# Attention and a feed-forward block on one core: the first two batches' q and k loaded in halves of 256 tokens, attention units of 192 tokens, the first chunk up-projected in column halves

## The chip, the cores and the metric

The kernel runs on one core of a Trainium2 chip. A core has a matrix engine (PE), a vector engine (DVE), a scalar engine (ACT), a general engine (POOL) and an engine that mostly issues loads and stores (SP). They run side by side, each through its own list of instructions in a fixed order, and wait for each other by semaphores. The metric is the device time of one execution in microseconds; less is better.

## The reference

Inputs are q, k and v (8 batches, 8 heads, 576 tokens, 64 per head, float32), w_in (512 x 2048) and w_out (2048 x 512).

```python
scores = scale * np.matmul(q, k.transpose(0, 1, 3, 2))
rel = pos[:, None] - pos[None, :]
mask_plain = (rel >= 0) & (rel < 32)
mask_dil = (rel >= 0) & (rel < 128) & (rel % 4 == 0)
# heads 0 to 3 take mask_plain, heads 4 to 7 mask_dil; softmax over the keys; times v
x = attn_out.transpose(0, 2, 1, 3).reshape(B * S, H * D)     # 4608 x 512
h = x @ w_in
out = np.maximum(0.01 * h, h) @ w_out                        # 4608 x 512, float32
```

Heads 0 to 3 ("plain", group 0) see the last 32 tokens, heads 4 to 7 ("dilated", group 1) every fourth of the last 128. Four tokens in a row are one step of the dilated heads, so all tokens of one residue modulo 4 attend among themselves.

## The kernel before

Everything is computed in float16 with float32 sums. The program is not written in the order in which it runs: every piece of work is handed to a small planner (`_Plan`, L62) as a task with an engine, an estimated duration, the tasks it depends on and a priority. `run` (L85) walks through time, gives each free engine the ready task of lowest priority number, and so fixes each engine's order; the instructions are then recorded in that order. Where the planner sees PE idle for over some 0.4 us in the head, matmuls on zeros are put in (L1595, after eight at the start, L1489): fillers, whose result nobody reads.

Attention is done batch by batch. Batches 0 and 1 (`EARLY`) take one path, the other six another one (`late_unit`, L945) which the change leaves as it is. On the early path `load_group` (L396) loads q and k of four heads, 512 tokens, with four tokens of one head (1 KB) as one piece and 128 partitions of four tokens; batch 0 in loads of two heads (256 KB), batch 1 in loads of four (512 KB). They land in float32 in the tiles `stg` and are cast into `nat` (L272). `turn` (L658) transposes them on PE (L692) into the bank `tp` or `fps`, and copies (L642, L644) bring them into `slots`: `qbd`, in which the two heads of a pair stand block-diagonally, and `kt`, the keys. The last 64 tokens of a batch follow by `load_rest` (L501), cast into `rest`.

A head pair of a batch is done in three units (`unit`, L807). Part 0 has the units 0 and 1, part 1 unit 2, with the last tokens. A plain unit covers 192 tokens in a row. A dilated unit 0 or 1 covers 96 steps of two residues, so that units 0 and 1 together need 384 tokens; unit 2 covers 48 steps of four residues. A unit's chain: a product on PE that adds the mask as a bias (L837, where `BY_PE` has the batch and part; elsewhere a mask is multiplied in afterwards on DVE or POOL, L874), the scores (L840 or L854), exp on ACT (L860), the product with the values and with ones (L886 to L918), the reciprocal as Ln and Exp on ACT (L930, L932) and the scaling into `xt` on DVE (L936). For batch 0's plain heads the values are loaded as they lie, cast into `pair` (the tile `pair1`), and brought into the windows that the units need by products with a spread identity (`permute`, L333).

`xt` holds x transposed, by chunks of 384 columns: for every two batches chunk 0 has the first 384 tokens of the even batch, chunk 1 those of the odd one, chunk 2 the last 192 of both. `up` (L1081) multiplies a chunk by w_in, 128 rows of the result at a time, four matmuls each (512 = 4 x 128), into one of two banks `hps`, and ACT writes it with the leaky ramp into `gt` (L1102). Chunk 0 is planned matmul by matmul (`BLOCKS`), so that it can begin before all of w_in is there. The rows 0 to 1023 of the result need the w_in blocks 0 to 3, the others the blocks 4 to 7. `down` (L1264, L1275) multiplies by w_out, and later `group` (L1315, L1364) does four tiles at once with seven products where eight would be plain.

Loads are issued by SP in the planner's order, which for the first two batches is given by the string `FIRST`: each sign is a group of loads (`b` q and k and `v` the values of a group of heads of batch 0, `c` and `y` of batch 1, `i` a block of w_in, `o` a block of w_out, 512 KB each, `0` and `1` the last tokens). Every load waits for the landing of the eighth load before it. `took` (L252) is the planner's estimate of a load's time, `LATE` what it adds to it for later loads, `AHEAD` how far it lets issues run ahead of the transfers, `RANKS` the priorities of the attention of the first two batches.

w_in and w_out arrive in float32 in tiles that are free early (`gt`, `wst`, `xt[1]`) and are cast in halves of 512 columns by `cast` (L265), on DVE or POOL; w_in's blocks 4 to 7 on POOL alone.

Of the kernel before, what the change touches and what calls it, by code (L numbers as in the profile page):

```python
# [9 lines left out]
FP16 = mybir.dt.float16  # L10
# [5 lines left out]
AHEAD, LATE = 5.0, 4.0  # L16
WHEN = (-5.0, 15.0, 46.0, 70.0, 100.0, 126.0, 160.0, 188.0)
CON = -1484.5
LOCK = 60.0
AFTER = -1495.0  # L20
FIRST = "bvbviiii0iiiicoocoyoooooy1"
RANKS = ((10.0, 6.0), (10.0, 0.5), (15.0, 2.0), (25.0, 2.0))


def _constants():
# [15 lines left out]
    d2 = (rel2 >= 0) & (rel2 < WIN)  # L41
    bias = np.where(np.concatenate([first, band, band, d0, d2], axis=1), 0.0, -60000.0)
    parts = [ident, bias, first, band, band, d0, d1, d1, d0, d2]
# [18 lines left out]
class _Plan:  # L62
# [22 lines left out]
    def run(self):  # L85
        free, waiting, lock = {}, {}, {}
        server = 0.0
# [12 lines left out]
        while len(order) < len(self.tasks):  # L100
            best = None
            for eng, cand in waiting.items():
# [3 lines left out]
                if eng == "SP":  # L106
                    here = max(here, server - AHEAD)
# [18 lines left out]
            if t.service:  # L126
                begin = max(at + t.dur + 0.9, server)
                server = begin + t.service
                t.done = server + 1.1 + t.late
            else:  # L130
                t.done = at + t.dur + t.lat
# [11 lines left out]
def kernel(  # L143
# [24 lines left out]
    TILED = ((0, 0), (0, 1), (1, 0))  # L168
    BY_PE = ((0, 0), (0, 1), (1, 0))
    POOL_MASK = (1,)  # L170
    BLOCKS = tuple(range(16))
    N_UPS = 8
# [20 lines left out]
    NBIAS, NMASK = 288 + 96 + 48, 288 + 288 + 48  # L193
# [3 lines left out]
    B_PL, B_D0, B_D2 = 128, 128 + 288, 128 + 288 + 96  # L197
# [47 lines left out]
    tpk = fps[1].bitcast(FP16)  # L245
# [6 lines left out]
    def took(n, size):  # L252
        for a, ta, b, tb in ((4, 9.0, 128, 15.0), (128, 15.0, 256, 19.0), (256, 19.0, 1024, 48.0),
                             (1024, 48.0, 2048, 85.0)):
            if size <= b:
                return n * (ta + (tb - ta) * (size - a) / (b - a)) / 16e3
        return n * size / 25.6 / 16e3

    def load(queue, dst, src, n, size, deps, prio, slow=1.0):
# [3 lines left out]
                        LATE if prio > -1500 + len(FIRST) else 0.8 if prio >= AFTER else 0.0)  # L263
# [35 lines left out]
    def clear_slots(slots, prio, deps):  # L299
        for i in slots:  # L300
            t_zero[i] = ([clear("DVE", qbd[i][64:128, 0:S], 0.34, 0.0, prio, deps),
                          clear("DVE", qbd[i][0:64, S:2 * S], 0.34, 0.0, prio, deps)],
                         [clear("DVE", kt[i][:, 0:PAD], 0.1, 0.0, prio, deps)])

    clear_slots(range(4), -2000, [])
    t_one = clear("POOL", ones, 0.1, 1.0, -1995)
    t_ones = {}
    TWO_ONES = float(np.ones(2, np.float16).view(np.float32)[0])

    def clear_ones(slots, deps, prio=-700):  # L310
        for i in slots:
            t_ones["d", i] = clear("POOL", at(vd[i].bitcast(FP32), 0, 128, D // 2, [64, 16], [1, D // 2]),
                                   0.48, TWO_ONES, prio,
                                   deps)
            t_ones["p", i] = clear("POOL", at(vp[i].bitcast(FP32), 0, 128, D // 2, [64, 12], [1, D // 2]),
                                   0.38, TWO_ONES, prio,
                                   deps)

    clear_ones(range(2), [], -1980)
    t_vr = [clear("POOL", vst[i][0:64, 1024:2048], 1.0, 0.0, -1970 + i) for i in range(2)]  # L320
    SPREAD, SHIFT = 36, 67

    def ident_at(tl, off, step, prio):
        t = clear("DVE", tl.bitcast(FP32), 0.3, 0.0, prio)
        return add("DVE", 0.2, 0.2, [t, t_id], lambda e: nc.vector.tensor_copy(
            out=at(tl, 0, 128, off, [step, 128]), in_=ident), prio)

    t_spread = ident_at(el[0], SPREAD, 4, -1985)
    t_shift = ident_at(el[1], SHIFT, 1, -1600)
    v_half = pair1  # L330
    permuted = []

    def permute(tiles, deps, prio, rest_from=None):  # L333

        if rest_from is None:
            n, b_users = tiles[0] // 2, []
            b_old = rings["TPK"][-1] if n else []
            bk = fps[n]
        else:
            n, b_old = ring("F", 2, b_users := [])  # L340
            bk = fps[n]

        def pe(e):
            for y, t in enumerate(tiles):
                for r in range(4):
                    s = 96 * t - 32 - r + SPREAD
                    nc.tensor.matmul(bk[:, 256 * y:256 * y + 256], el[0][:, s:s + 128],  # L347
                                     at(v_half, 0, 128, r * D, [256, 4], [1, D]),
                                     start=(y == 0 and r == 0), stop=(r == 3), skip_group_check=True)
                if t == 5:  # L350
                    for r in range(4):
                        for i in range(2):
                            nc.tensor.matmul(bk[:, 256 * y + 128 * i:256 * y + 128 * i + 128],
                                             el[1][0:64, 3 - r:131 - r],
                                             at(turned[i], 0, 64, r * D, [256, 2], [1, D]),
                                             start=False, stop=(r == 3), skip_group_check=True)
        t_p = add("PE", 0.11 * (4 * len(tiles) + 4 * (5 in tiles)), 0.25,
                  deps + b_old + [t_spread] + [t_shift] * (5 in tiles), pe, prio)
        permuted.append((t_p, b_users))
        res = []  # L360
        for j in range(2):
            vt = vp[j]

            def fn(e, j=j, vt=vt):
                o = at(vt, 0, 128, tiles[0] * 128, [768, 2], [128, 2], [1, D])
# [5 lines left out]
            t = add((("ACT", 0.3), ("DVE", 0.36)), None, 0.2, [t_p] + kept_old[j], fn, prio)  # L371
            b_users.append(t)
            res.append(t)
        if rest_from is None:
            rings["F"][n].extend(res)
# [4 lines left out]

    kept, v_late, seen_ones = {}, {}, {}
    kept_old = [[], []]

# [1269 lines left out]
```

## Time and profile before

| | |
|---|---|
| median of 3 runs | 306.08 us (305.56 to 306.25) |
| the profiled execution | 306.29 us, its span 304.50 us |
| PE busy | 294.4 us (97%), 2970 matmuls |
| DVE busy | 231.0 us (76%) |
| ACT busy | 188.7 us (62%) |
| POOL busy | 132.3 us (43%) |
| moved by DMA | 51.09 MB, 168 GB/s in the mean |

The span runs from the first to the last instruction; 1.79 us of the profiled execution lie around it. A busy PE is not always at useful work: the fillers count. The rows of a timeline have the start, the time from the first start to the last end of a run of like instructions, the engine, the line, the operation, what it writes and reads, and in brackets the idle time before it and what ended it. PE's matmuls overlap, so the pace of a run is read from the starts. SPq is SP issuing a load.

### The profile page before, as it was taken

The page shows a single profiled execution, that of the slowest core. Times are in us where ns is not written, and L with a number is a line of the kernel's source. Part 1 is how long each engine was busy: PE and PEld are TensorE (multiplying, and loading weights), DVE is VectorE, ACT ScalarE, POOL GpSimd, SP SyncE. Part 2 cuts the span into 40 slices and gives each one's busy share as a digit, 9 for nine tenths or more (in the row PEclk, how much of TensorE's full clock was granted, in tenths as well). Part 3 has the DMA queues.
Part 4 walks back from the last instruction along what each step waited for, and adds up shares of the span by engine and source line. Part 5 has one row for each costly group of instructions (what it writes and reads, how often), then busy time and mean ns, then how long its engine had stood idle before and what let it go on. Part 6 is the DMA issues. An engine that isn't in the chain of part 4 may idle for free.

```text
span 304.5 us, 7869 instructions
## 1 busy us (share of the span) xinstructions
PE 294.4 (97%) x2970; PEld 225.4 (74%) x2970; DVE 231.0 (76%) x478; ACT 188.7 (62%) x458; POOL 132.3 (43%) x179
## 2 busy tenths in 40 slices
PE   6889999999999999997999999999999999999994
PEld 3646655667777676786777777887788999999984
DVE  6875875689686869959888779879775899697552
ACT  3857854795556678464766567456565688767230
POOL 5469555393674949159094668665000000000000
PEclk9999999999999999999999999999999999999999
DMA  7999999999999899976999969793102110031124
GB/s 241 404 370 392 407 289 201 239 201 167 253 171 196 190 188 196 174 180 134 183 161 221 204 136 194 159 208 80 37 2 72 34 37 2 11 91 32 32 76 146
DMA packets 160390, 51.09 MB, mean 168 GB/s; under 512 B 137632, under 2 KB 157024, under 8 KB 160352
## 3 DMA queue, kind: packets, MB, share of 16 engines
q1 hardware_dynamic: 159520, 49.86, 68.3%
q10 hardware_dynamic: 832, 0.73, 0.8%
q8 instruction: 23, 0.38, 0.5%
q14 instruction: 15, 0.12, 0.1%
HBM read 41.13 MB, written 9.44 MB: 166 GB/s over the span
## 4 chain that ended last, share of the span: by engine, by line
PE 90%; DVE 5%; ACT 3%; DMA 1%; issue 1%; DVEq 0%
PE hps L1091 29%; PE fps L1364 26%; PE fps L1275 9%; PE ops L1015 3%; PE hps L1188 3%; PE ops L1188 3%; PE ops L1063 2%; PE sps L1188 2%; PE tp L1188 1%; PE tp L692 1%; PE ops L1364 1%; PE tp L982 1%; PE sps L982 1%; DVE ee L1008 1%; PE fps L347 1%; PE tp L975 1%
## 5 line engine op out<-in xcount | busy, mean ns | idle before, releaser
L1091 PE MATMUL hps<-xt,w_in 128*128 128x384 f16 (+1 forms) x640 | 111.7, 310 | 0.8 <-DVE w_in L272 0.6
L1102 ACT ACTIVATE gt<-hps 128x384 f16<-128x384 f32 (+1 forms) x160 | 72.8, 461 | 43.8 <-PE hps L1091 41.5
L1091 PEld LDWEIGHTS <-w_in 128*128 128x128 f16 x640 | 56.7, 98 | 26.3 <-DVE w_in L272 1.0
L1364 PEld LDWEIGHTS <-gt 128*128 128x128 f16 x672 | 64.4, 98 | 9.7
L679 POOL COPY slots<-turned 64x576 f16<-64x576 f16 x48 | 36.3, 757 | 47.4 <-DVE turned L674 45.5
L1364 PE MATMUL fps<-w_out,gt 128*128 128x256 f16 x416 | 53.6, 273 | 0.0
L272 POOL CAST nat<-stg 128x576 f16<-128x576 f32 (+1 forms) x53 | 43.0, 834 | 9.7 <-DMA stg<-in_q_dram 3.5
L1275 PE MATMUL fps<-w_out,gt 128*128 128x512 f16 x128 | 32.4, 379 | 0.0
L1037 DVE TENSOR_TENSOR rc<-ops,recs 96x384 f16<-96x384 f32 x48 | 25.7, 538 | 0.3
L1393 ACT COPY stg<-fps 128x512 f32<-128x512 f32 (+1 forms) x24 | 12.8, 532 | 14.4 <-PE fps L1364 14.4
L1008 DVE TENSOR_TENSOR ee<-ee,con 128x576 f16<-128x576 f16 x24 | 17.2, 722 | 3.5 <-ACT ee L994 3.5
L1033 DVE RECIPROCAL recs<-ops 96x6 f32<-96x6 f32 x48 | 8.7, 181 | 14.7 <-PE ops L1015 12.5
L1401 DVE TENSOR_TENSOR osb<-fps,stg 128x512 f32<-128x512 f32 x18 | 12.4, 687 | 9.7 <-PE fps L1364 5.6
L272 POOL CAST vd<-v_all 128x1024 f16<-128x1024 f32 (+2 forms) x20 | 18.0, 918 | 2.7 <-DMA v_all<-in_v_dram 2.7
L1211 ACT ACTIVATE gt<-stg 128x384 f16<-128x384 f32 x36 | 18.0, 524 | 1.1 <-DVE stg L1205 1.1
L1275 PEld LDWEIGHTS <-gt 128*128 128x128 f16 x128 | 11.6, 98 | 9.1
L644 DVE COPY slots<-tp 64x128 f16<-64x128 f16 (+7 forms) x42 | 13.4, 333 | 6.3 <-PE tp L692 5.6
L674 DVE STREAM_TRANSPOSE turned<-nat 128x576 f16<-128x576 f16 x24 | 17.7, 751 | 0.0
L685 DVE STREAM_TRANSPOSE slots<-nat 128x576 f16<-128x576 f16 x24 | 17.7, 745 | 0.0
L1008 DVE TENSOR_TENSOR el<-el,con 128x576 f16<-128x576 f16 x24 | 15.0, 630 | 2.7 <-ACT el L994 2.5
L1188 PEld LDWEIGHTS <-w_in 128*128 128x128 f16 x192 | 16.4, 98 | 0.5 <-DVE w_in L1119 0.3
L994 ACT ACTIVATE ee<-sps 128x288 f16<-128x288 f32 x24 | 9.8, 409 | 8.4 <-PE sps L982 5.8
(158 smaller groups left out, 529.3 us busy)
## 6 DMA issues: line engine op xcount, KB each, us to landing
stg<-in_q_dram SPq DMA_DIRECT2D x48, 144.0 KB, 3.2
stg<-in_k_dram SPq DMA_DIRECT2D x48, 144.0 KB, 2.9
v_all<-in_v_dram SPq DMA_DIRECT2D x24, 256.0 KB, 3.8
v_all<-in_v_dram SPq DMA_DIRECT2D x24, 192.0 KB, 3.2
gt<-in_moe_w_in_dram SPq DMA_DIRECT2D x5, 512.0 KB, 7.1
out_dram<-osb SPq DMA_DIRECT2D x22, 96.0 KB, 2.0
out_dram<-osb SPq DMA_DIRECT2D x40, 48.0 KB, 1.8
out_dram<-osb SPq DMA_DIRECT2D x25, 64.0 KB, 2.2
```

The costliest lines, as they stand in the source:

```text
L272: ENG[e].tensor_copy(out=dst, in_=src)
L674: lambda e: nc.vector.transpose(xb, na[:, 0:S]), prio)
L679: lambda e, p0=p0, hh=hh: nc.gpsimd.tensor_copy(out=at(qb, p0, p0 + 64, hh * S + o, *od), in_=at(xb, p0, p0 + 64, i, *id_)), prio, 0.0, "m ...
L685: lambda e: nc.vector.transpose(kb[:, PAD:PAD + S], na[:, S:2 * S]), prio)
L1008: nc.vector.tensor_tensor(out=x, in0=x, in1=mk, op=ALU.mult)
L1037: nc.vector.tensor_tensor(out=at(xb, 0, 96, 768 * n + 64 * i, [256, 3], [128, 2], [1, D]), in0=at(ot, 0, 96, 0, [130, 3], [65, 2], [1, D]) ...
L1091: nc.tensor.matmul(ht[:, 0:n], at(w_in, 0, 128, i * DFF + j // 2 * 256 + j % 2, [2, 128]), at(xt[m % 2], 0, 128, i * 1152 + x0, *dims), st ...
L1102: lambda e: nc.scalar.activation(out=gt[c % NG][:, j * n_c + x:j * n_c + x + n], in_=ht[:, 0:n], func=AF.Prelu, alpha=0.01),
L1188: nc.tensor.matmul(cell[:, n * z:n * z + n], lhs(2 * p + z, i), rhs(i), start=first and z == 0 and i == 0, stop=z == 1 and i == 1, skip_gr ...
L1211: lambda e: nc.scalar.activation(out=at(g, 0, 128, j * n_c + n * y, [n_c, 2], [1, n]), in_=at(src, 0, 128, 0, [n, 2], [1, n]), func=AF.Pre ...
L1275: nc.tensor.matmul(ft, g[:, j * n_c + tt * 128:j * n_c + tt * 128 + 128], w_out[:, j * DM:j * DM + DM], start=(j == 0), stop=(j == NJ - 1))
L1364: nc.tensor.matmul(bk[:, x:x + HN], tl[:, off + j * step:off + j * step + 128], rhs(j), start=first and x == 0 and j == 0, stop=j == HJ - ...
```

## The change

Batches 0 and 1 are handled in three thirds. Part 0 of the loads has tokens 0 to 255 of all heads, part 1 tokens 256 to 511, and the rest follows as before. A load has now two of a group's four heads and 64 pieces of four tokens, 128 KB, with the two heads in alternating partitions, so that a transpose of 128 partitions gives two heads at once, interleaved by columns. After each part comes one unit of every head pair: unit t is now the tokens 192t to 192t + 191 for all heads, and a dilated unit has 48 steps of four residues. `load_part`, `load_values`, `turn_part`, `turn_rest` and `attend_third` replace the early branches of `load_group`, `turn` and `attend`; `permute` is called once for each unit and uses `tp` and `fps[1]` in turn, and the second score bank of units 1 and 2 of batch 0 is `fps[0]`. The tiles' clears on DVE now cover the whole `kt` of the slots 0, 1, 4 and 5. `up_half` does chunk 0, and chunk 2 of the first two batches, in halves of 192 columns: chunk 0's first half has the columns of unit 0, its second half those of unit 1. The casts of batch 0 may go to DVE, ACT or POOL. `FIRST`, `RANKS` and `LATE` have new values, `took` new figures, and the planner lets only eight loads be under way in the first 60 us of its time.

```diff
-AHEAD, LATE = 5.0, 4.0
+AHEAD, LATE = 5.0, 2.5
+FLIGHT = 8
-FIRST = "bvbviiii0iiiicoocoyoooooy1"
-RANKS = ((10.0, 6.0), (10.0, 0.5), (15.0, 2.0), (25.0, 2.0))
+FIRST = "AaiBiiiCiiiiooooDEdooooF"
+RANKS = ((-30.0, 5.0), (-8.0, 0.1), (-6.0, 0.1), (-4.0, 0.1), (-3.0, 0.1), (20.0, 2.0))
...
-                    here = max(here, server - AHEAD)
+                    here = max(here, server - AHEAD, lands[-FLIGHT] if here < LOCK else 0.0)
...
-                         [clear("DVE", kt[i][:, 0:PAD], 0.1, 0.0, prio, deps)])
+                         [clear("DVE", kt[i][:, 0:PAD + (S if i in (0, 1, 4, 5) else 0)],
+                                0.33 if i in (0, 1, 4, 5) else 0.1, 0.0, prio, deps)])
...
-        t = load("SP", st, src, 128, 4096, old, prio, 1.3 if n < 4 else 1.0)
+        t = load("SP", st, src, 128, 4096, old, prio)
...
-        u_lo, u_hi = ((0, 96) if u < 2 else (96, 144)) if dil else (48 * u, 48 * u + 48)
+        u_lo, u_hi = 48 * u, 48 * u + 48
...
+    def four_heads(queue, st, x, src, base, deps, prio):
+        return [load(queue, st[:, x + 256 * c:x + 256 * c + 256],
+                     dram(src, base + c * HS, [4 * D, 64], [2 * HS, 2], [1, 256]),
+                     128, 1024, deps, prio) for c in range(2)]
+
+    def load_part(b, h, prio):
+
+        for g in (1, 0):
+            base = (b * H + 4 * g) * HS + 256 * h * D
...
+            for o, src in ((0, q), (1, k)):
+                rank = prio + 0.4 * (1 - g) + 0.1 * o
+                lo = four_heads(K_QUEUE if o and (b, h) == (0, 0) else "SP", st, 512 * o, src, base,
+                                s_old, rank)
+                c_qk.append(cast(at(na, 0, 128, 512 * o, [D, 2], [128, 4], [1, D]),
+                                 at(st, 0, 128, 512 * o, [256, 2], [D, 4], [1, D]), 512,
+                                 lo + n_old, rank, ("DVE", "ACT", "POOL") if b == 0 else CENG))
...
+    def turn_part(b, h, g, prio):
+
+        dil = g == 1
+        na, c_qk, n_users = turned_in[b, h, g]
+        bk, p_old, p_users = turn_bank(b)
+        tp = [add("PE", 0.23, 0.25, [c_qk[o], t_id] + p_old, turn_in(bk, na, 4, 4 * o), prio, 0.2)
+              for o in range(2)]
...
+        ev = [move(at(qbd[tn], 64 * hh, 64 * hh + 64, hh * S + 64 * h, [2 * S, 2], [144, 4], [1, 64]),
+                   at(bk, 64 * hh, 64 * hh + 64, 0, [1, 2], [128, 4], [2, 64]), 512,
+                   tp[:1] + (old if h == 0 else []) + z[0], prio, eng) for hh in range(2)]
...
+    def up_half(c, y, p, done, acc):
...
+        x0, x_in, x_out = ((48 * y, [[96, 4], [1, 48]], [[48, 4], [1, 48]]) if c == 0 else
+                           (384 + S * y, [[1, 192]], [[1, 192]]))
+
+        def part_of(i):
+            def fn(e):
+                for z in range(2):
+                    nc.tensor.matmul(ht[:, 192 * z:192 * z + 192],
+                                     at(w_in, 0, 128, i * DFF + p * 256 + z, [2, 128]),
+                                     at(xt[0], 0, 128, i * 1152 + x0, *x_in),
+                                     start=(i == 0 and z == 0), stop=(i == NI - 1 and z == 1),
+                                     skip_group_check=True)
+            return fn
...
+    UP_AT = {0: (0.0, 5.2), 2: (12.0, 45.0)}
+    UPS = (((0, 0, 0),), ((0, 0, 4), (0, 1, 0), (0, 1, 4)), ((2, 0, 0), (2, 0, 4)))
...
+    def attend_third(b, t, first, step):
+        names = ("ABC", "DEF")[b]
+        if t < 2:
+            load_part(b, t, ranks[names[t]])
+            if t == 0:
+                load_values(b, ranks[names[t].lower()])
+            new = {g: turn_part(b, t, g, first + step * (1 - g) * 2) for g in (1, 0)}
+        else:
+            load_rest(b, ranks[names[t]])
+            new = turn_rest(b, first)
...
+        for n, hp in enumerate((2, 3, 0, 1)):
+            dn = v_slot[b, hp][0]
+            unit(b, hp, t, moved[b, hp // 2], v_deps[b, hp] + (
+                [t_one] if (b, t) in BY_PE else [t_ones["d" if hp >= 2 else "p", dn]]),
+                first + step * n)
```

In the new `FIRST`, `A` and `B` are the two halves of batch 0's q and k, `a` its values, `C` its last tokens, `D`, `E`, `d` and `F` the same of batch 1. `K_QUEUE` is SP.

## The prediction

> **What bounds the kernel now.** I read the windows first, then the PE timeline of the first 25 us, then what stands beside it on DVE, POOL and SP. All instructions, then those on the tile of the filler matmuls alone:
>
> ```profile
> 0.00:5.39 5.39, 3.71 (x10) 1.28 (x11) 3.75 (x17) 1.73 (x2) 3.85 (x12) 1.00 0.61 188
> 5.39:22.00 16.61, 13.84 (x142) 8.84 (x143) 13.63 (x37) 11.32 (x33) 8.36 (x14) 1.00 1.05 385
> 22.00:50.00 28.00, 28.00 (x257) 16.97 (x256) 18.88 (x49) 17.78 (x48) 19.60 (x34) 1.00 1.04 336
> 50.00:299.50 249.50, 247.69 (x2557) 197.54 (x2555) 193.91 (x374) 157.92 (x377) 100.53 (x121) 1.00 0.64 134
> ...
> 5.39:22.00 16.61, 3.48 (x12) 0.97 (x12) 0.00 (x0) 1.00 1.05 385
> ```
>
> Columns: stretch, its length, busy time of PE, PEld, DVE, ACT, POOL, granted clock, DMA share, GB/s (the last line has PE, PEld, POOL only). From 22.0 to 299.5 us PE is idle 1.81 us in all: it is the bound, and time can only come from less PE work or from the head. In the head the first real matmul starts at 5.39; from there to 22.0 PE is idle 16.61 - 13.84 = 2.77 us and runs 3.48 us of fillers (matmuls on zeros, 12 of them), 6.25 us without real work. DMA is full (1.05) from 5 us on. What ends the head:
>
> ```profile
> 18.47 0.42 DVE L272 CAST w_in<-wst 128x512 f16<-128x512 f32 x1
> 18.96 0.61 POOL L272 CAST w_in<-wst 128x512 f16<-128x512 f32 x1 [1.84 <-DMA wst<-in_moe_w_in_dram]
> 19.09 1.16 PE L1091 MATMUL hps<-xt,w_in 128*128 128x384 f16 x6
> 19.51 1.04 POOL L272 CAST rest<-stg 128x1024 f16<-128x1024 f32 x1
> 19.67 1.16 DVE L272 CAST w_in<-wst 128x512 f16<-128x512 f32 x1
> 20.89 0.50 PE L1091 MATMUL hps<-xt,w_in 128*128 128x384 f16 x2 [0.64 <-DVE w_in L272]
> ```
>
> The first six up matmuls start when the last attention result is written (19.1); the fourth w_in block lands at 18.9 (POOL's cast of its other half waits for it until 18.96), and the half that they need waits on DVE behind other work and takes 1.16 instead of 0.42 us, so block four is used at 20.89. Two things therefore end together: attention on 512 tokens and w_in.
>
> ```profile
> 0.74 0.45 SPq L262 DMA_DIRECT2D stg<-in_q_dram  x1
> 1.24 0.47 SPq L262 DMA_DIRECT2D stg<-in_k_dram  x1
> 1.76 0.47 SPq L262 DMA_DIRECT2D stg<-in_q_dram  x1
> ...
> 139.54 2.95 DVE L1008 TENSOR_TENSOR ee<-ee,con 128x576 f16<-128x576 f16 x1
> ...
> 140.16 2.02 POOL L272 CAST vd<-v_all 128x1024 f16<-128x1024 f32 x2
> ...
> 142.55 0.36 PE L1015 MATMUL ops<-vp,ee 128*128 128x65 f16 x6 [1.60 <-DVE ee L1008]
> ```
>
> SP issues one load per 0.51 us; and 1.6 of the later 1.81 us are one mask on DVE that took 2.95 us while POOL cast.
>
> **The change, part by part.** The sum is made against the profiled execution: 306.29 us, a span of 304.50 and 1.79 around it; the median shown is 306.08, 0.21 less.
>
> *Smaller attention steps, earlier chunk.* Chunk 0's first half now needs units of 192 tokens, not 512. In the built order PE has 10 fillers behind the opening eight instead of 14; before the first transposes 1 instead of 2, so 9 instead of 12 in the stretch above. Each stood for 6.25 / 12 = 0.52 us without work, the waits around it included; 9 of them make 4.7, a gain of 1.6. Why it can be had: units 0 and 1 wait for their own 256 tokens, up matmuls of two banks run with the first blocks of w_in, and the half of block four that the first ups need is cast on POOL (PE waits for POOL there), where 0.61 is the whole price. Ends: the block could land at 16.04 + 1.28 = 17.3 (POOL's casts that waited for blocks one to three start at 13.48, 14.76 and 16.04) and be cast by 17.9 instead of 20.84, a gain of 3.0; or it lands 0.5 later than now, POOL casts it by 20.0 and the rest of the tokens by 21.05 (1.04 more), for which PE now waits before its next ups, then the two `turned` casts (0.80, 0.61) and eight w_in casts (0.57 each), so that block eight's first half is ready at 21.05 + 1.41 + 7 x 0.57 = 26.4. The order has an up on that block only some 7 us of PE work behind block four, so PE catches up with POOL and the gain is eaten: +0.3. I take -1.6, which lies between.
>
> *PE work added.* Chunk 0: 128 matmuls of 192 columns instead of 64 of 384. Eight of 384 take 1.30 (21.80 to 23.10), two of 192 take 0.165 (49.78 to 49.95): 128 x 0.0825 - 64 x 0.1625 = +0.16. Eight dilated units (two head pairs, units 0 and 1, two batches) take eight 64x48 value products where four 64x96 stood: from their start to the next task 0.33 (30.50 to 30.83) against 0.29 (43.79 to 44.08), +0.04 x 8 = +0.32; their scores, 4 x 96 against 2 x 192 columns, 0.17 both. PE is the bound, so +0.5 counts, except what falls into gaps of the head. Transposes (80), bias products (20) and spread products (32) keep their number.
>
> *Loads in halves.* Batch 0's q and k are 16 loads of 128 KB (8 of 256 KB before), batch 1's 16 instead of 4 of 512 KB; v, w_in and w_out are issued as before in size. The first eight take 8 x 0.51 = 4.1 us to issue; the last of them, issued at 4.3, lands 2.5 to 3.0 later (the 32 KB and the 108 KB load of constants took that from issue to landing), so the first megabyte is in at about 7.1, against 6.69 now, when DVE casts the last of it: the stream starts 0.4 to 0.5 us late, which is in the ends above. Batch 1: 16 x 0.51 = 8.2 us for 2.1 MB, which at a 512 KB block per 1.28 takes 5.1: up to 3.0 us that everything behind them slips, the second half of w_out (POOL's cast that waits for its last block starts at 42.32 now) first, and v of batch 1 with it. An issue also waits for the landing of the eighth load before it, so pieces of 128 KB keep at most 1 MB under way. Cover: chunk 2's first half, 64 x 0.0825 = 5.3 us of PE work, which stood behind 53 us, now comes before; so slip costs little, from 0 to +3.0. I take +0.2, for single waits of batch 1's casts, which PE now meets close behind their landing. The Trainium skill, DMA: Bandwidth & Descriptors, Measured (HBM->SBUF, 128 partitions), asks for loads of 1 MiB and gives 0.95 us for 64 KB, 6.15 for 1 MB, so by it 32 pieces would cost far more than their bytes. This trace shows what speaks against it: loads overlap, blocks of 512 KB land 1.28 us apart though one takes 7.1 from issue to landing (the median of five).
>
> *On DVE and POOL.* Four of the six key tiles are now cleared whole (128x304 instead of 128x16, two early, two later): 4 x some 0.25 (an estimate from the 64x288 row, 0.30) = 1.0 us, less one memset of 0.35 and one copy; the early two are hidden because the first q cast moves from DVE to ACT, which sits idle until 4.95; the later two stand before w_in casts on DVE, whose halves of blocks three and four are not the ones that PE meets first. If that cover goes, +0.6.
>
> *Planner constants* reorder loads, casts and PE work for later batches; no instruction is added. 1.81 us idle there now; 0 to twice that. I take no change.
>
> Sum: -1.6 + 0.5 + 0.2 = -0.9: 305.4 against 306.29, as a median **305.2 us**.
>
> **The rivals.**
>
> *A much earlier start.* Block four lands at 17.3, x of the first half is done well before, and PE goes through: -3.0 + 0.5, and part of the later 1.81 goes as well: 303.0. For it: a unit's chain from its score to x took 7.13 to about 11.0. Against: DMA share 1.05; the bytes ahead of block four are the same 5.2 MB.
>
> *Nothing gained.* PE catches up with POOL's casts as in the worse end: +0.3, or with the added work already in it 306.3. For it: POOL is busy 5.00 of 5.00 us from 20 to 25 now, and PE was never behind those casts so closely.
>
> *Slower: batch 1's loads become the bound.* Place: 30 to 50 us. Price: -0.9 turned to -1.6 + 0.5 + 3.0 = +1.9, 308.0. It decides once the last w_out block slips past what chunk 2's half covers, or v of batch 1 lands behind the place of its value products. For it: PE has no wait at all in 22 to 50 now, so every slip is new. Against: the 5.3 us moved ahead. It is what the DMA rule above would make of the time.
>
> *Slower: DVE and POOL collide elsewhere.* The mask above lost 2.95 - 0.72 = 2.2 us; two such places instead of one make +2.0 - 0.9: 307.2. The Trainium skill, SBUF - State Buffer, Who interferes with whom, says that a DVE instruction with two SBUF inputs and a GpSimd one that reads SBUF hold a port pair in turn, for a whole instruction; by that rule, with the order of loads re-dealt, such stalls move by chance, and the trace agrees in this one place.
>
> *The change does not do what it says* can be left out: the built order shows the halves.
>
> **How the numbers follow.** Earlier by the sum: 0.36. Much earlier: 0.20. Nothing gained: 0.16. Loads bound: 0.20. Collisions: 0.08. A measurement tells some 0.2%, 0.6 us, from no change, so faster means below 305.5. Of the sum's 0.36 (its own range 304.3 to 306.0) 0.26 lie below and 0.10 within; of nothing gained 0.10 within, 0.06 above. Faster 0.26 + 0.20 = 0.46, within 0.10 + 0.10 = 0.20, slower 0.06 + 0.28 = 0.34. Range: down to 302.6, where the head's 3.0 and half a later microsecond go; up to 308.6, the loads at 3.0 with a head that gains only 1.0.
>
> **What would show it.** Right: the first up matmul before 17 us and the second batch of ups behind no filler; idle and fillers from the first transposes to 22 us at 4 to 5 us; PE full from 22 to 50. Wrong: PE waits for POOL's w_in casts near 25 us (nothing gained), waits for casts of batch 1 or w_out between 30 and 50 us (loads), or a long DVE mask beside a POOL cast ahead of a PE gap (collisions). The landings of w_in's fourth and eighth block (18.9 now; POOL casts the eighth from 25.15) and of the last w_out block (42.3) decide between them.

## The result, and the profile after

The changed kernel takes 319.02 us (median; 317.49 to 322.26), the kernel before, run beside it, 305.95 (305.56 to 306.25): a ratio of 1.0411, 95% interval 1.035 to 1.0472. The prediction was 305.2 us, at most 308.6; sign and size were wrong. A ratio is taken over the runs within 1.5% of a kernel's fastest, so where the runs of a kernel lie far apart its median is above what the ratio says.

The profiled execution took 317.87 us, its span is 316.1 (before: 304.5). The same windows as before (stretch, length, busy time of PE, PEld, DVE, ACT, POOL, granted clock, DMA share, GB/s), and those of the filler tile alone:

```profile
0.00:5.39 5.39, 4.45 (x14) 1.63 (x14) 3.73 (x14) 1.90 (x2) 3.85 (x12) 1.00 0.50 140
5.39:22.00 16.61, 12.30 (x140) 8.53 (x138) 10.70 (x26) 10.52 (x28) 3.81 (x6) 1.00 0.92 288
22.00:50.00 28.00, 25.85 (x297) 20.68 (x298) 17.20 (x44) 17.48 (x46) 13.86 (x26) 0.88 0.94 305
...
5.39:22.00 16.61, 3.12 (x9) 0.86 (x8) 0.00 (x0) 1.00 0.92 288
```

Three things differ. The loads: 140 and 288 GB/s in the first two stretches, 188 and 385 before. The fillers: nine, as foretold, but PE is idle for 16.61 - 12.30 = 4.31 us beside them (2.77 before), so 7.43 us of the head are without work, not 4.7. And the granted clock, 1.00 throughout before, is 0.88 from 22 to 50 us. In finer windows, with the PE timeline beside them:

```profile
22.00:24.00 2.00, 0.71 (x8) 0.65 (x9) 0.97 (x3) 0.71 (x3) 0.86 (x1) 1.00 1.08 280
24.00:26.00 2.00, 1.14 (x8) 0.59 (x6) 1.32 (x5) 0.49 (x1) 1.30 (x2) 0.50 1.02 360
26.00:28.00 2.00, 2.00 (x20) 1.48 (x19) 0.09 (x1) 1.80 (x5) 2.00 (x4) 0.50 1.03 387
...
30.00:32.00 2.00, 2.00 (x25) 1.24 (x23) 0.39 (x3) 0.55 (x2) 2.00 (x4) 0.80 1.04 420
```

```profile
21.18 0.25 PE L794 MATMUL ops<-ee,ones 128*64 128x192 f16 x2
23.29 0.51 PE L1024 MATMUL hps<-xt,w_in 128*128 128x192 f16 x4 [1.86 <-DVE w_in L272]
...
25.63 0.82 PE L1024 MATMUL hps<-xt,w_in 128*128 128x192 f16 x4 [0.86 <-POOL w_in L272]
...
59.59 0.62 PE L658 MATMUL tp<-con,rest 128*128 128x128 f16 x8 [1.66 <-POOL rest L272]
...
191.32 0.42 PE L923 MATMUL ops<-vd,el 128*128 128x65 f16 x8 [1.31 <-DVE el L916]
...
213.01 0.35 PE L923 MATMUL ops<-vp,ee 128*128 128x65 f16 x6 [2.91 <-DVE ee L916]
```

PE waits 1.86 us for w_in's third block and 0.86 for the fourth; then the clock is at 0.50 from 24 to about 30.8, and the same four ups take 0.82 us instead of 0.51. Later it waits for the last tokens of batch 1 (`rest`) and, at 190 and 210 us, for masks on DVE. On POOL, and on SP before and after:

```profile
22.84 0.86 POOL L272 CAST w_in<-wst 128x512 f16<-128x512 f32 x1 [1.38 <-DMA wst<-in_moe_w_in_dram]
24.70 0.87 POOL L272 CAST w_in<-wst 128x512 f16<-128x512 f32 x1 [0.99 <-DMA wst<-in_moe_w_in_dram]
```

```profile
8.04 1.07 SPq L262 DMA_DIRECT2D wst<-in_moe_w_in_dram  x2
```

```profile
0.74 1.35 SPq L262 DMA_DIRECT2D stg<-in_q_dram  x2
2.13 1.25 SPq L262 DMA_DIRECT2D stg<-in_k_dram  x2
3.42 1.25 SPq L262 DMA_DIRECT2D stg<-in_q_dram  x2
...
14.41 0.90 SPq L262 DMA_DIRECT2D wst<-in_moe_w_in_dram  x2
```

The fourth w_in block lands at 24.65 (POOL's cast that waits for it starts at 24.70), 5.75 us later than before. SP issues one load per 0.65 us (two in 1.29), not 0.51; 128 KB per 0.65 us is 202 GB/s, about half of what the stream reached before. From 0.7 to 12.4 us SP issues without waiting for anything, while DMA moves 212 GB/s from 3 to 9 us (365 before): there the issuing is the bound. The third and fourth w_in blocks, which stand behind all 16 small loads, are issued from 14.41 us on instead of 8.04, 6.4 us later, which accounts for the 5.75 by which the fourth lands late. The values of batch 1 follow: POOL casts the first of them at 47.05 instead of 35.95 us, and PE reads them at 47.74; the last w_out block is cast from 56.59 on instead of 42.32.

Where the 11.6 us of span went, from these windows: idle and fillers from 5.39 to 60 us 11.24 us (4.31 + 3.12 + 2.15 + 1.66) against 6.25, +5.0; idle of PE from 60 to 215 us 155.00 - 150.78 = 4.22 against 1.77, +2.4; PE busy some 5.9 us at half the clock, +3.0; added PE work +0.5, an estimate of the prediction that no run measured apart. That leaves 0.7 unplaced. Counted over the whole span, PE is busy without its fillers 299.3 - 7.3 = 292.0 us, before 294.4 - 7.2 = 287.2, so +4.8; 3.0 of that are the clock, and the added work can be up to 1.8.

### The profile page after: what moved, and what is told of

It reads as the page before. It is cut to its first block, busy times and chain, and to the rows that moved or that the text cites. A ratio compares the mean times of both kernels' runs of the same rounds, so it can differ in the third digit from the quotient of the medians.

```text
span 316.1 us, 8094 instructions
## 1 busy us (share of the span) xinstructions
PE 299.3 (95%) x3078; PEld 232.5 (74%) x3078; DVE 228.6 (72%) x479; ACT 188.4 (60%) x446; POOL 127.0 (40%) x172
## 4 chain that ended last, share of the span: by engine, by line
PE 68%; DMA 14%; SPq 8%; POOL 3%; DVE 3%; issue 2%; ACT 1%; POOLq 0%
PE fps L1302 21%; PE hps L998 19%; PE fps L1211 8%; SPq L262 8%; DMA stg<-in_k_dram 4%; DMA v_all<-in_v_dram 3%; PE ops L1124 3%; PE hps L1124 3%; PE ops L923 3%; DMA gt<-in_moe_w_out_dram 3%; DMA wst<-in_moe_w_in_dram 3%; DMA gt<-in_moe_w_in_dram 2%; PE sps L1124 2%; PE hps L1024 2%; PE ops L971 2%
## 5 line engine op out<-in xcount | busy, mean ns | idle before, releaser
L998 PE MATMUL hps<-xt,w_in 128*128 128x384 f16 x448 | 87.0, 326 | 0.0
L1005 ACT ACTIVATE gt<-hps 128x384 f16<-128x384 f32 x112 | 55.2, 494 | 36.4 <-PE hps L998 34.4
L998 PEld LDWEIGHTS <-w_in 128*128 128x128 f16 x448 | 40.4, 98 | 19.7
L272 POOL CAST nat<-stg 128x576 f16<-128x576 f32 (+1 forms) x49 | 35.5, 749 | 28.3 <-DMA stg<-in_q_dram 14.6
L539 POOL COPY slots<-turned 64x576 f16<-64x576 f16 x48 | 37.1, 773 | 13.4 <-DVE turned L534 11.6
L1024 PE MATMUL hps<-xt,w_in 128*128 128x192 f16 x256 | 26.9, 252 | 3.0 <-DVE w_in L272 2.2
L272 POOL CAST vd<-v_all 128x1024 f16<-128x1024 f32 (+2 forms) x18 | 20.8, 1163 | 15.0 <-DMA v_all<-in_v_dram 11.6
L1024 PEld LDWEIGHTS <-w_in 128*128 128x128 f16 x256 | 21.1, 100 | 4.7 <-DVE w_in L272 2.6
L1331 ACT COPY stg<-fps 128x512 f32<-128x512 f32 (+1 forms) x24 | 12.8, 534 | 13.1 <-PE fps L1302 12.7
L510 DVE COPY slots<-tp 64x128 f16<-64x128 f16 (+2 forms) x35 | 14.6, 437 | 8.0 <-PE tp L658 6.1
L1035 ACT ACTIVATE gt<-hps 128x384 f16<-128x384 f32 x32 | 15.6, 491 | 7.0 <-PE hps L1024 6.7
L902 ACT ACTIVATE ee<-sps 128x288 f16<-128x288 f32 x24 | 9.9, 412 | 12.4 <-PE sps L890 11.2
```

What stands on the lines that cost most here:

```text
L272: ENG[e].tensor_copy(out=dst, in_=src)
L539: lambda e, p0=p0, hh=hh: nc.gpsimd.tensor_copy(out=at(qb, p0, p0 + 64, hh * S + o, *od), in_=at(xb, p0, p0 + 64, i, *id_)), prio, 0.0, "m ...
L998: nc.tensor.matmul(ht[:, 0:n], at(w_in, 0, 128, i * DFF + j // 2 * 256 + j % 2, [2, 128]), at(xt[m % 2], 0, 128, i * 1152 + x0, *dims), st ...
L1005: lambda e: nc.scalar.activation(out=gt[c % NG][:, j * n_c + x:j * n_c + x + n], in_=ht[:, 0:n], func=AF.Prelu, alpha=0.01),
L1024: nc.tensor.matmul(ht[:, 192 * z:192 * z + 192], at(w_in, 0, 128, i * DFF + p * 256 + z, [2, 128]), at(xt[0], 0, 128, i * 1152 + x0, *x_in ...
```

## Experiments

Theory at the start: the loads of 128 KB throttle the stream of the head (one SP issue each, at most eight under way), so w_in, batch 1 and w_out come late; the gap then costs clock; the waits at 190 and 210 us are a matter of their own. Rivals: the alternation of heads makes the transfers slow; the new order of work is at fault; the planner's constants are.

### The size of the loads

**e1**, before, with small loads:

```diff
-lo = [load("SP", at(st, 0, 128, j * 512, [256, 2], [1, 256]), ... [4 * D, 128], [HS, 2], [1, 256]), 256, ...) for j in range(2)]
+lo = [load("SP", at(st, 0, 128, j * 256, [1, 256]), ... [4 * D, 128], [1, 256]), 128, ...) for j in range(4)]
```

> The kernel before, its attention, chunks and order kept, but the q and k loads of the first two batches cut into pieces of 128 KB (32 loads where there were 12). Theory (loads of 128 KB throttle the stream: SP needs one issue for each, and at most eight are under way): 309 to 313 us, w_in's fourth block lands after 20.5 us instead of 18.9, GB/s from 0 to 15 us well below 380. Rival (the size of the loads does not matter, the new order of attention and ups does): 305.5 to 307 us, fourth block near 19.

309.20 us (308.27 to 310.02), ratio 1.0102 [1.0075, 1.0129]. The fourth block landed at 22.21. Small loads alone cost 3.0 us (the before beside it took 306.19), with the old attention, chunks and prices. Its window and SP's queue:

```profile
5.39:22.00 16.61, 11.92 (x130) 7.56 (x131) 10.50 (x29) 11.40 (x31) 5.32 (x9) 1.00 0.97 311
```

```profile
1.66 0.91 SPq L262 DMA_DIRECT2D stg<-in_k_dram  x2
2.62 0.91 SPq L262 DMA_DIRECT2D stg<-in_q_dram  x2
```

One issue per 0.48 us here: a 128 KB load of one head is cheaper to issue than one of two alternating heads (0.65), and still 131 KB / 0.48 us = 273 GB/s. An issue pace that is harmless for 256 KB (0.51 us: 514 GB/s) binds for half of it.

**e2**, the changed kernel, pairs joined:

```diff
-return [load(queue, st[:, x + 256 * c:x + 256 * c + 256], dram(src, base + c * HS, [4 * D, 64], [2 * HS, 2], [1, 256]), 128, ...) for c in range(2)]
+return [load(queue, at(st, 0, 128, x, [256, 2], [1, 256]), dram(src, base, [4 * D, 64], [2 * HS, 2], [HS, 2], [1, 256]), 256, ...)]
```

> The changed kernel with each pair of 128 KB loads of a half (two heads each) joined into one load of 256 KB with the same bytes, rows and places: 16 issues less. Theory (issues and the eight under way throttle the head): 311 to 314 us, w_in's fourth block lands before 21.5 us instead of 24.65, the 2.06 us gap of PE at 21.2 shrinks and the granted clock stays 1.0 from 24 to 31 us. Rival (what is slow is the pattern, two heads alternating over the partitions, not the number of loads): 317 to 320 us, fourth block still after 23.5. Rival (planner's order): 317 to 320 us, fourth block before 21.5.

309.80 us (306.77 to 312.94), ratio 1.0081 [1.0038, 1.0123]: 9.2 us back, more than expected. Fourth block at 20.02, clock 1.00 throughout in the profiled execution (307.28 us), and PE waits for no w_in block up to 22 us. The alternation was kept, so it alone is not what is slow; it does make an issue dearer (0.65 us against the 0.48 of e1).

```profile
5.39:22.00 16.61, 13.68 (x155) 9.70 (x153) 10.98 (x30) 11.96 (x33) 5.13 (x10) 1.00 1.04 341
```

```profile
1.59 0.62 SPq L262 DMA_DIRECT2D stg<-in_k_dram  x1
2.26 0.62 SPq L262 DMA_DIRECT2D stg<-in_q_dram  x1
```

Each issue is still 0.62 long, but moves twice the bytes: 341 GB/s instead of 288. Yet the head is not shorter than before: 2.93 us idle and 3.26 of fillers from 5.39 to 22, 6.19 against 6.25, and 0.93 idle from 22 to 50 against none.

**e6**, joined for batch 0 alone (the old pair of loads kept where `base >= H * HS`):

> The changed kernel with the 128 KB loads joined in pairs for batch 0 alone; batch 1 keeps its 16 loads of 128 KB. Theory (the head's small loads cost some 4 us of PE waits and 3 us of clock, batch 1's small loads the wait of 1.8 us at 57.7 us, and the rest is the order of the later stores): 311 to 313 us, clock 1.0 from 20 to 32 us, PE still waits over 1 us between 50 and 62 us. Rival (batch 1's 16 loads are the costly ones, by keeping w_out and v behind them): 315 us or more.

316.34 us (312.66 to 316.59), ratio 1.0305 [1.0248, 1.0363]: between theory and rival. The clock held and a wait over 1 us stayed between 50 and 60 us (1.2, for `rest`), as the theory said; but PE also idled 4.26 us from 60 to 215 us, as much as in the changed kernel (4.22), where e2 has 0.60, and that is about the missing part.

**e4**, `K_QUEUE = "ACT"`:

> The changed kernel with the four k loads of batch 0's first 256 tokens issued by ACT's queue instead of SP's. Theory (SP's 0.65 us per issue limits the first 5 us): the first megabyte lands 1 to 1.5 us earlier, the first real matmul comes 0.5 to 1 us earlier, total 317 to 318.5 us. Rival (the transfers are slow by themselves): landings and total as in the changed kernel, 319 us.

318.69 us (317.19 to 319.79), ratio 1.0425 [1.0395, 1.0455]: no gain. The stream did rise (293 GB/s from 5.39 to 22, 288 in the changed kernel; fourth block at 24.12), but ACT issued instead of casting: PE waited 2.5 us for `nat` from ACT. With fewer loads to issue, SP now waited 4.1 us for landings before 13.7 us, where the changed kernel waited 0.7, and issued the third and fourth w_in blocks from 14.39 on, no sooner than there (14.41). So the limit of eight under way lies close behind the pace of the issues.

**e7**, heads stacked:

```diff
-dram(src, base + c * HS, [4 * D, 64], [2 * HS, 2], [1, 256])
+dram(src, base + c * HS, [2 * HS, 2], [4 * D, 64], [1, 256])
...
-at(bk, 64 * hh, 64 * hh + 64, 0, [1, 2], [128, 4], [2, 64])
+at(bk, 64 * hh, 64 * hh + 64, 0, [64, 2], [128, 4], [1, 64])
```

> The changed kernel with the two heads of a load stacked (first head on partitions 0 to 63, second on 64 to 127) instead of alternating; as many loads of as many bytes, and the copies out of PSUM read runs of 64 instead of every second column. Theory (it is the bytes under way, eight loads of 128 KB, not the alternation): issues may fall from 0.65 to about 0.5 us, w_in's fourth block still lands after 23 us, total 317.5 to 319.5 us. Rival (the alternation is what makes issue and transfer slow): 310 to 314 us.

387.70 us (384.69 to 389.19), ratio 1.2632 [1.2563, 1.27]. Neither foresaw it. From 8 to 20 us, and on SP:

```profile
8.00:20.00 12.00, 1.83 (x10) 0.98 (x10) 0.75 (x2) 1.57 (x3) 0.00 (x0) 0.50 0.14 48
```

```profile
0.73 1.32 SPq L262 DMA_DIRECT2D stg<-in_q_dram  x2
2.10 5.12 SPq L262 DMA_DIRECT2D stg<-in_k_dram  x2
7.26 5.31 SPq L262 DMA_DIRECT2D stg<-in_q_dram  x2
```

The first two loads are issued in 0.66 us each, as in the changed kernel; then SP gets rid of one per 2.68 us (two in 5.36), which is the pace of the transfers (131 KB / 2.68 us = 49 GB/s). The DMA share is 0.14, about two of the 16 engines. The Trainium skill, DMA: Bandwidth & Descriptors, Why a DMA increments its semaphore by 16 and not by 1, says that the slowest dimension of the pattern sets how many engines a DMA uses; with a slowest dimension of 2 that would be two engines, and the trace agrees. So the alternating order of the change, 64 groups outermost, is the one that spreads; the pattern that looks simpler costs 69 us.

### The clock

**e5**, eight fillers in the gap at 21.2 us:

```diff
+late = next(t for t in pe if t.kind == "U" and any(d is w_in_t[0][2] for d in t.deps))
+for i in range(8):
+    w = _Task((("PE", 0.01),), 0.0, [], idle(512, fps[0]), 0, 0.0, -8 + i, "w")
```

> The changed kernel with eight more fillers (128x512 on zeros) on PE just ahead of the up matmuls that wait for w_in's third block, so in the 2.06 us gap at 21.2 us; nothing else differs. Theory (the gap itself makes the granted clock fall to 0.50 for 6.7 us, which costs PE some 3 us more than the gap): clock 1.0 from 20 to 32 us, total 315.5 to 317 us. Rival (the clock falls for another reason, or PE waits for w_in there in any case, so nothing is won): 318 to 320 us.

319.49 us (318.11 to 321.08), ratio 1.0438 [1.0396, 1.0479]. The windows show both halves of the answer, and the timeline why:

```profile
24.00:26.00 2.00, 1.54 (x15) 1.00 (x13) 1.78 (x6) 0.49 (x1) 1.32 (x3) 1.00 1.00 363
26.00:28.00 2.00, 1.81 (x27) 1.48 (x27) 0.47 (x2) 1.70 (x5) 2.00 (x4) 1.00 1.02 401
...
46.00:48.00 2.00, 0.59 (x8) 0.36 (x5) 1.50 (x4) 0.62 (x2) 0.07 (x1) 1.00 1.19 314
...
50.00:52.00 2.00, 2.00 (x16) 1.78 (x16) 1.02 (x3) 1.17 (x4) 1.00 (x3) 0.50 1.00 369
```

```profile
48.60 0.31 PE L800 MATMUL ops<-ee,vd 128*64 128x48 f16 x8 [2.01 <-POOL vd L272]
```

With the gap filled the clock stayed at 1.00 from 24 to 32 us, so the gap is what made it fall there (one execution of each kernel). But PE, 1.8 us ahead at 30 us (the same score products start at 29.80 instead of 31.63), met batch 1's `vd` before it was cast, waited 2.01 us, and lost the clock there (and once more behind a wait of 2.25 us at 212). The gain was given back at the next late load: in the changed kernel, too, PE reads this `vd` only 0.7 us after POOL begins to cast it, so the loads of batch 1 are the bound behind those of the head.

**e12**, joined loads and fillers (five at 15.1 us, three at 28.9):

> The changed kernel with the loads of both batches joined in pairs and eight more fillers on PE in two of the gaps of the head that are left (five ahead of the second transposes at 15.1 us, three ahead of the value products at 28.9 us). Theory (the spread of 306.8 to 312.9 us with joined loads is the granted clock, which falls or not after gaps of 1 to 2 us): all runs within 306 to 308.5 us, clock above 0.997 in each. Rival (the spread comes from the transfers, the clock follows): spread of some 5 us and a median near 310 us stay.

312.71 us (306.63 to 314.81), ratio 1.0106 [1.0062, 1.015]. The rival holds: the profiled execution had the clock at 1.00 throughout and took 312.29, with 155.00 - 150.01 = 4.99 us of PE idle from 60 to 215, where e2's execution of 307.28 has 0.60. Between these two, the spread of joined loads lies in the later waits.

### The later waits

**e3** (`LATE` 4.0), **e8** (joined, `LATE` 4.0):

> The changed kernel with the planner's lateness of loads (LATE) back at 4.0 from 2.5; the first eight batches' loads are the same. Theory (the two waits of 1.3 and 2.9 us at 190 and 210 us come from loads queued behind 14 stores on SP because LATE lets the planner trust late loads): 315 to 317 us, no PE wait over 1 us between 180 and 215. Rival (these stalls have another cause): 318 to 320 us, stalls stay. The head must not change: gap at 21 to 23 us as before.

> The changed kernel with the loads joined in pairs (both batches) and LATE back at 4.0. Theory (the two causes add up, and what is left of the change is its earlier chunk, 0.5 us more PE work and a little clock): 305 to 308 us, no wait over 1 us after 60 us. Rival (the rest of the loss lies in the order of the head): 309 to 311 us as with joined loads alone.

e3: 315.75 us (three of four from 314.01 to 317.13, one 347.72), ratio 1.0298 [1.0246, 1.035], the time that the theory gave, without its reason: a wait of 2.9 us at 184 us took the place of those at 190 and 210. e8: 311.79 us (309.40 to 316.94), ratio 1.0159 [1.0098, 1.022], no better than joined loads alone, with waits at 100 and 168 us.

**e9** and **e10** (joined), later stores partly on ACT's queue:

```diff
-store(ob, HN * x, c, tt, col * HN, HN, [t], o_users)
+store(ob, HN * x, c, tt, col * HN, HN, [t], o_users, True)
```

> The changed kernel with part of the later stores (every piece of a tile's store but the first, from the tiles of 256 columns on) issued by ACT's queue instead of SP's, so that fewer stores stand ahead of loads on SP. Theory (the PE waits of 1.5 and 3.1 us at 190 and 210 us are loads of the last batches queued behind stores on SP): no PE wait over 1 us from 150 to 230 us, total 314 to 316.5 us, head as in the changed kernel. Rival (the waits come from DVE and POOL blocking one another, or from the transfers): waits stay, 318 to 321 us.

> The changed kernel with the loads of both batches joined in pairs and part of the later stores on ACT's queue. Theory (small loads and loads behind stores are the two causes, they add up): 305.5 to 308.5 us, PE full from 60 to 300 us but for under 1 us. Rival (what is left of joined loads' loss lies in the head): 309 to 311 us. To beat the kernel before it would have to come under 305.5.

334.18 us (331.19 to 335.58), ratio 1.0882 [1.0828, 1.0937], and 317.50 (317.26 to 320.57), ratio 1.0393 [1.0343, 1.0443]: both far worse. SP's own waits from 60 to 260 us in e9 (us in all, times, longest):

```profile
SPq L262 <- DMA out_dram<-osb: 34.1, 12, 11.8
```

Eleven of these twelve waits end with the landing of a store that ACT issued. So the eight under way are counted over both queues: a store that stands late on ACT holds up SP's loads. In the changed kernel SP waits for no store from 60 to 215 us.

**e11**, six loads moved ahead of 14 stores near 191.75 us:

> The changed kernel with one block of the SP queue turned round: the last six loads of q and k (two of q, four of k) that stand behind 14 stores near 191.75 us are issued ahead of them. Nothing else is moved. Theory (the PE wait of 3.07 us at 210 us is these loads behind the stores): that wait falls under 0.6 us, the wait of 1.5 us at 190 stays, total 315.5 to 317.5 us. Rival (the wait is made by DVE and POOL, or the slots of these loads come free only then): the wait stays over 2 us, 318 to 320 us.

318.58 us (316.50 to 320.01), ratio 1.039 [1.0336, 1.0444]. The wait at 210 us fell to 0.21, as the theory said, and the time did not follow: waits of 2.09, 0.83 and 0.70 us stood at 168 to 178 us, ahead of the edit, where the changed kernel's profiled execution had none. Such places move between kernels whose order differs only ahead of them (e5 has 2.25 us at 212 and none of 0.5 us at 190), so moving one block proves its own wait only. What made that wait can be read in the changed kernel, on POOL and DVE:

```profile
208.89 1.28 POOL L272 CAST nat<-stg 128x576 f16<-128x576 f32 x2 [2.98 <-DMA stg<-in_k_dram]
```

```profile
209.59 0.78 DVE L545 STREAM_TRANSPOSE slots<-nat 128x576 f16<-128x576 f16 x1 [3.40 <-POOL nat L272]
...
212.07 0.88 DVE L916 TENSOR_TENSOR ee<-ee,con 128x576 f16<-128x576 f16 x1
```

POOL waits for loads of k, DVE for POOL; then DVE works without a pause up to the mask, which is not a long one (0.88 us, not 2.95), and PE goes on at 213.01.

What differs much between the two kernels is how long POOL waits for loads of q and k between 60 and 215 us. Before, then after:

```profile
POOL nat L272 <- DMA stg<-in_k_dram: 2.4, 2, 2.0
POOL nat L272 <- DMA stg<-in_q_dram: 1.1, 1, 1.1
```

```profile
POOL nat L272 <- DMA stg<-in_q_dram: 14.6, 6, 4.3
POOL nat L272 <- DMA stg<-in_k_dram: 12.2, 5, 3.2
```

3.5 us against 26.8. The planner's prices (`LATE` 2.5 for 4.0, 0.3 for 0.8 us on the first loads, a new table in `took`) order these loads. They alone were exchanged:

> The kernel before with the changed kernel's planner prices alone (LATE 2.5, the new table of transfer times, 0.3 us for the first loads); SP's order is the same over its first 44 rows. Theory (these prices make the planner place later loads with too little lead, so POOL's casts wait for them): POOL waits over 10 us for q and k loads between 60 and 215 us instead of 3.5, PE waits 2 to 5 us there, total 307.5 to 311 us. Rival (the new structure leaves the loads no lead, the prices do not matter): 305.5 to 307 us, POOL's waits under 8 us.

> The changed kernel with the planner prices of before (LATE 4.0, old table, 0.8 us), its small loads kept. Theory (prices): PE waits after 60 us fall from 4.7 to under 2 us, 314.5 to 317 us. Rival (structure): 316 to 320 us with waits of 2 us and more after 60 us.

> The changed kernel with joined loads and the planner prices of before. Theory (prices): 305.5 to 308.5 us, spread under 3 us, POOL waits under 10 us for q and k loads between 60 and 215 us. Rival (structure): 308 to 312 us with a spread of 4 us or more, POOL's waits 12 to 30 us as with the new prices.

**e13**: 309.51 us (307.44 to 310.00; before beside it 305.69), ratio 1.0114 [1.0077, 1.0151]. The theory holds: POOL waits 24.1 us, PE idles 155.00 - 150.76 = 4.24 from 60 to 215, though the head became shorter (1.73 idle and 3.11 of fillers, 4.84 against 6.25).

```profile
POOL nat L272 <- DMA stg<-in_q_dram: 16.4, 6, 5.0
...
POOL nat L272 <- DMA stg<-in_k_dram: 7.7, 5, 3.5
```

**e14**: 312.31 us (312.00 to 312.74), ratio 1.0221 [1.0204, 1.0238]; 6.7 us back, more than expected, PE idle 0.31 from 60 to 215 us, all runs within 0.8 us. But POOL still waits 11.8 + 8.0 = 19.8 us for q and k there: its waits alone do not hold PE up. The prices are shown to make PE's later waits, not that POOL's waits are the path. **e15**: 309.81 us (309.38 to 310.44), ratio 1.0138 [1.012, 1.0156]; POOL waits 5.5 us and the spread is small, as the theory said, the time is the rival's. What is left there, 4.1 us (before beside it 305.69), is the new structure with loads of 256 KB. In its profiled execution, whose span is 3.3 us longer than the kernel's before, PE idles 2.1 us more, runs 0.8 us less of fillers, and is busy 2.0 us more with the rest.

The prices apart, in the kernel before (the table only together with the 0.3):

> The kernel before with LATE 2.5 instead of 4.0 alone. Theory (LATE 2.5 trusts later loads too much, and POOL's and DVE's order meets them too early): 308 to 310 us, head as before (11.3 us without real work by 20 us). Rival (the table or the shifted head makes the waits): 305.5 to 307 us.

> The kernel before with the lateness of its first loads 0.3 instead of 0.8 us alone. Theory (this shortens the head, LATE makes the later waits): 304.2 to 305.4 us, one filler less, head 10.3 us without real work by 20 us instead of 11.3. Rival (any new order of the later loads brings waits of its own): 306 to 309 us.

> The kernel before with 0.3 us for the first loads and the new table of transfer times, LATE kept at 4.0. Theory (LATE alone makes the later waits): 304.2 to 305.7 us. Rival (the table is at fault too, or any new order of later loads brings waits): 307 to 310 us.

**e16**: 303.76 us (303.56 to 306.18), ratio 0.9919 [0.9891, 0.9947], against the theory and faster than both kernels. The profiled execution is the slowest of the five (306.18; the others 303.56 to 303.94), so its trace does not show the gain; it does show that PE idles 0.06 us from 60 to 215, where it idled 1.77 before, though POOL waits 9.9 us for q and k:

```profile
60.00:215.00 155.00, 154.94 (x1603) 116.71 (x1601) 121.71 (x242) 101.27 (x251) 92.89 (x117) 1.00 0.89 180
```

**e17**: 306.05 us, ratio 0.9998 [0.9984, 1.0012]: one filler less and 4.97 us without work from 5.39 to 22 instead of 6.25, given back between 50 and 60 us, where PE idles 0.77 us, and in two waits at 141 and 195. **e18**: 306.53 us, ratio 1.0023 [0.9993, 1.0054], but three of its ten executions took 308.6 to 309.1. So neither `LATE` nor the 0.3 alone makes the later waits; the 0.3, with the table or without, does nothing that the medians show, `LATE` alone gains 2.5 us, and the three together lose 3.8. The table alone, and its pairing or that of the 0.3 with `LATE`, were not tried.

The medians in one table (us; the loads of e1 have one head each, those of the new structure two in alternation):

| | old prices | new prices |
|---|---|---|
| structure before, loads as before | 306.1 | 309.5 (e13) |
| structure before, loads of 128 KB | 309.2 (e1) | |
| new structure, loads of 256 KB | 309.8 (e15) | 309.8 (e2) |
| new structure, loads of 128 KB | 312.3 (e14) | 319.0 |

## Why the prediction was wrong

- *Loads in halves* (taken at +0.2, ends 0 and +3.0) is the first step that failed. It put the first megabyte 0.4 to 0.5 us late and took that for all of the delay in the head. But the w_in block that ends the head stands behind 16 small loads, not eight: 16 x 0.65 = 10.4 us of issues against 8 x 0.51 = 4.1, 6.3 us more, and SP came to the third and fourth blocks 6.4 us later. Small loads cost 3.0 us in the kernel before (e1), 2.5 in the new structure with old prices (e14 less e15), 9.2 with the new ones (319.0 less e2). The working took 0.51 us per issue from loads of 256 KB; these took 0.65. And it did not ask whether the stream keeps its rate: 288 GB/s instead of 385.
- The rule that the prediction weighed and set aside (the Trainium skill, DMA: Bandwidth & Descriptors, Measured: loads of 1 MiB; its table is of loads issued by GpSimd, these come from SP) pointed the right way. "Loads overlap" was read from blocks of 512 KB; with eight under way that is 4 MB, with 128 KB it is one. Up to 12.4 us it was not this limit that held the stream but the issuing.
- *Smaller attention steps* (-1.6, ends -3.0 and +0.3). The worse end let the fourth block land 0.5 us late; it was 5.75. The number of fillers was right and worth nothing: they stand where the planner expects a wait, while the real waits stood elsewhere. With joined loads (e2) the head has 6.19 us without work to 22 us against 6.25, so the gain is about nil even then. Of the signs of being right none came: the first up starts at 19.59 us (forecast before 17; 19.09 in the kernel before), the head has 7.4 us without work (forecast 4 to 5), and PE is not full from 22 to 50. PE's wait of 0.86 us for POOL at 25.6, the sign of *nothing gained*, is there, but POOL itself was waiting for the landing.
- *Planner constants* (no change, at most twice 1.81 us) is the second step that failed: +3.8 us by themselves (e13), +6.7 with small loads (e14), and nothing with loads of 256 KB in the new structure (e2 and e15, 309.8 both).
- The rival *batch 1's loads become the bound* (308.0) had the right mechanism: the values of batch 1 slip by 11.1 us and the last w_out block by 14.3, far more than the 3.0 that it allowed and the 5.3 us of moved ups that were to cover it; e5 shows PE waiting for them at 46 to 49 us. It was mis-sized, and its place began earlier, in the head; in the changed kernel, late already, PE has no wait from 26 to 57 us.
- The granted clock was in no step and no rival: 3.0 us in the profiled execution.
- The rival *DVE and POOL collide elsewhere* named masks on DVE, and PE does wait for masks at 190 and 210 us; but they take 0.43 and 0.88 us, and the one at 210 is late by its loads (e11).
- *On DVE and POOL* the step held: at 22.8 us DVE had been idle for 1.5 us, waiting for the landing of w_in's third block, when it cast it; the memsets of key tiles ahead of that cost nothing. The +0.5 of PE work stays an estimate: without fillers PE is busy 1.3 to 2.0 us more than before in four executions of the new structure (e8, e12, e2, e15), but 1.7 more in e13 as well, which has the old one.

What stays open: the causes do not add up (small loads 3.0, prices 3.8, structure 4.1, together 10.9 of 13.1 us), and of the later waits it is shown only that prices and size of loads make them together; but for the one at 210 us it is not shown which load in which place.

## What to carry to other kernels

Cut a load only after comparing its bytes per issue with the rate that the stream holds: at half the bytes and a dearer pattern, the queue that issues becomes the bound, and everything behind it is late, also what was not touched. Constants of a scheduler are part of a change like any instruction: exchange them alone, and one at a time, before the rest is judged. When a filled gap brings nothing, look for the next late load rather than doubt the gap.

## What the runs showed of the hardware

- The granted clock fell to 0.50 after a gap of 1.86 us in which and around which PE was thinly busy (0.71 of 2.00 us), and stayed there for some 6.8 us; in e5 after a gap of 2.01, for some 3.4 us. After the gap of 2.91 us at 213 in the changed kernel (PE busy 1.09 us from 210 to 214) it stayed at 1.00, so the length of one gap does not decide. The Trainium skill, TensorE: Matmul & The Clock Gate, Part 1, speaks of an idle window of about 3.4 us; here shorter gaps were enough, and the measurement decides.
- Issuing a load of 128 KB took 0.48 us for one head over 128 partitions, 0.65 for two alternating heads; where the outermost dimension was two, 0.66 for the first two loads and 2.68 for later ones, the pace of the transfers.
- The limit of eight loads under way couples queues: SP waited 34.1 us for stores, in eleven of twelve cases stores of ACT's queue (e9).
